# Projection first on SyncE's queue, warming operand set by VectorE, orders made anew

## The chip, the cores and the metric

The kernel runs on one core of one Trainium2 chip. The metric is device time in microseconds, the median of three executions. The core has five instruction streams that run in parallel and meet by semaphores: TensorE (PE: products; PEld: its weight loads), VectorE (DVE), ScalarE (ACT), GpSimd (POOL) and SyncE (SP), which here only issues transfers.

## What is computed

Attention in which a query sees only the keys of its own hash bucket, followed by a feed-forward layer with a squared ReLU:

```python
q_bits = (np.einsum('bhsd,dk->bhsk', q, proj) > 0).astype(np.int64)
k_bits = (np.einsum('bhsd,dk->bhsk', k, proj) > 0).astype(np.int64)
...
mask = q_bucket[:, :, :, None] == k_bucket[:, :, None, :]
scores = scale * np.matmul(q, k.transpose(0, 1, 3, 2))
scores = np.where(mask, scores, -1000000000.0)
...
attn = attn / (np.sum(attn, axis=-1, keepdims=True) + 1e-09)
return np.matmul(attn, v).astype(np.float32)
...
h = np.maximum(x @ w_in, 0.0)
return (h * h @ w_out).astype(np.float32)
```

Batch 4, 8 heads, 768 tokens, head size 64, 6 hash bits (`proj` is 64 x 6); 3072 tokens through 512 x 2048 x 512. All in float32.

## The kernel before

**Work.** A visit is one batch, one pair of heads and 384 queries; there are 32 visits of 6 units. A unit is 128 queries of one head against all 768 keys: TensorE makes the scores `pS`, in which the hash codes are extra rows of the product (tiles `A`, `L` against `Q`, `M`, or `arena` for batch 0); VectorE takes the maximum (`e<-pS`), ScalarE the exponential (`e<-e,maxes`) with its row sum in `sums`; the sum is inverted (`rv`). For the first five visits (`PLAIN_AV`, line 54) GpSimd multiplies by `rv` (`e<-e,rv`), TensorE transposes in six pieces of which three at a time lie in a bank (`bank<-unit_f,e`, `pT<-unit_f,e`), and ScalarE copies them out (`aT<-bank`, `aT<-pT`). For the others ScalarE and VectorE split the scaled row into two float16 parts (`hl`), and a transposing transfer brings it to `aT`. After six units TensorE multiplies with the values (`pA<-aT`), and the tile is copied out (`xx<-pA`). When the four pairs of heads of 384 tokens are there, `moe` (from line 1171) multiplies by the first weights (`bank<-xx,win`), squares (`g`), and multiplies by the second (`po<-wo,g`). The last batch goes through `strassen`, with fewer products.

**Setting up a pair of heads.** `prep` makes the hash codes `bits` (a product with the projection `pj`, compared with a threshold), scales `R` into `A`, makes `L`, copies a scaled half of `A` over its other half (`A<-A`, or `arena<-arena`, 64 x 768: the half copy; engines in `HALF_BY`, line 75), and puts the codes, 12 rows by 384, into `L` and `M` (`code`; engines in `CODE_BY`, line 75). The weights come in pieces of 512 columns: a transfer, then `top` on ScalarE, the bit merge `f` on VectorE, the high part `win<-f` or `wo<-f` and the low part `win<-f,win`.

**The start.** The first visit has a path of its own: keys `K` and queries `G` are loaded in halves (`T` and `U`), the projection `pj0` goes into `pj` and `wide_pj` on VectorE, and TensorE multiplies K and G by `wide_pj` (`pd<-K,wide_pj`, `pd<-G,wide_pj`). `GS` is G scaled by ScalarE; `pS<-K,GS` are the first scores. The transfers of this path stand in a list (lines 636 to 643) whose entries follow each other on each queue. Before them `emit` puts warming products `bank<-ones`, whose operand `ones` is filled by a memset, and more of them wherever the planned order leaves TensorE without work for long before the first feed-forward product (`fill`, from line 518).

**The order.** No order is written by hand: every operation is recorded by `Program.add`, and `Program.order` plays a list schedule with durations of its own (`cost`, `LAGS`, `PRICE`), taking ready operations by rank; where an operation may run on several engines, the one that would be done first takes it. `MOVES` is a table of 150 entries that shift ranks of stretches of the list. So a changed parameter or table changes the order on every engine. Lines 532, 536 and 539 are where `emit` issues warming products, grouped products and everything else, which is why almost every row of the profile has line 539.

Of the kernel before, what the change touches and what calls it, by code (L numbers as in the profile page):

```python
# [12 lines left out]
BF16 = mybir.dt.bfloat16  # L13
# [10 lines left out]
P = 128  # L24
B, H, S, D = 4, 8, 768, 64
NB = 6
# [15 lines left out]
PRICE = dict(pe=1, dve=4.53, act=0.28, pool=2.55, sp=6.14)  # L42
AHEAD, DELAY, LAG = 101, 21166, 1.0
# [4 lines left out]
PREP, STACKS, VALUES = -3, 2, 1  # L48
WIN_RANK, WOUT_RANK = (12, 3.1999999999999997), (27, 1.6)
# [11 lines left out]
EARLY_SUMS, SUMS_RANK, SUMS_AT = 24, 160, (68, 42)  # L61
VERIFY = (3, 7)

PT_TAGS = ('pm', 'po2')

WIN_AT, WOUT_AT = (0, 1), 0
FIRST = len(WIN_AT)

PACE = ((16, 0), (64, 141), (96, 277), (125, 480), (157, 537), (188, 622))

TOP_BY, LOW_BY = ('act',), ('dve',)
RUN = 18
MERGED, TOGETHER, PAIRED = 0, 1, 0
LANES = 8
CODE_BY, HALF_BY, WIDE, KM = (('dve', 'gp'), ('sp',)), ('dve',), 1, 76
# [7 lines left out]
IDLE_FROM, IDLE_FIRST, IDLE_SHARE, IDLE_UNTIL = 1000, 36, 0.6, 18000  # L83
# [477 lines left out]
def run(ctx: ExitStack, tc, kq, v, proj2, w_in, w_out, consts, out, flag):  # L561
    fast = flag is not None
# [5 lines left out]
    pr = Program(tc)  # L568
# [50 lines left out]
    cst = sb([P, 4], F32, "cst")  # L619
    if not fast:  # L620
        sp.dma_start(cst, consts[:, 0:4])
    pj = sb([P, 32], F32, "pj")
    dve.memset(pj, 0.0)
    ones = sb([P, P], BF16, "ones")
    (pool if fast else dve).memset(ones, 1.0)
# [60 lines left out]
    for x in tops:  # L686
        dve.memset(x.bitcast(F32), 0.0)
# [728 lines left out]
```

## Time and profile before

| | |
|---|---|
| three executions | 790.21, 790.21, 790.88 us, median 790.21 |
| the profiled execution | 792.51 us, its span 790.4 us |
| granted TensorE clock | 0.999 of full |
| TensorE (PE) busy | 773.9 us, 98% |
| VectorE (DVE) busy | 644.8 us, 82% |
| ScalarE (ACT) busy | 621.3 us, 79% |
| GpSimd (POOL) busy | 273.0 us, 35% |

The span goes from the first to the last instruction of the profiled execution; 2.11 us of its time lie outside. Busy times are of one engine; in a row with a time in brackets the engine stood idle before that instruction, and what ended the wait stands behind the arrow. Instructions of one engine overlap slightly, so that the distance of two starts is shorter than the length shown.

### The profile page before, as it was taken

The numbers are of one execution on the slowest core, as the hardware profiler recorded it, in microseconds if no ns is written. First come the engines' busy times: TensorE is split into PE (matmuls) and PEld (weight loads), VectorE is DVE, ScalarE is ACT, GpSimd is POOL, SyncE is SP. The second block draws the span as 40 slices with busy tenths as digits, with TensorE's granted clock in tenths as the row PEclk, the third lists the DMA queues.
The fourth block names the chain that finished last, engine by engine and source line by source line (L and its number), as shares of the span: only waits on it lengthen the run. The fifth ranks groups of instructions, "written<-read, shape, count | busy, mean of one in ns | idle before, by whom it ended". The sixth has DMA issues, their size and how long they took to land.

```text
span 790.4 us, 14405 instructions
## 1 busy us (share of the span) xinstructions
PE 773.9 (98%) x4893; PEld 421.9 (53%) x4893; DVE 644.8 (82%) x1265; ACT 621.3 (79%) x1164; POOL 273.0 (35%) x357
## 2 busy tenths in 40 slices
PE   8999999999999999999999999999999999999996
PEld 5555645555555555555555555545555555545553
DVE  6999999989999889888888888888988546967462
ACT  6999999999889889989888897979867779432211
POOL 3766422433414242441415243233582011320000
PEclk9999999999999999999999999999999999999999
DMA  7876699999999999999999989988626698830002
GB/s 227 255 222 194 195 239 191 224 200 191 184 190 184 190 182 193 203 192 185 191 191 196 179 176 207 183 164 167 114 41 141 174 291 256 258 101 0 1 1 84
DMA packets 286273, 137.41 MB, mean 174 GB/s; under 512 B 258912, under 2 KB 266352, under 8 KB 286192
## 3 DMA queue, kind: packets, MB, share of 16 engines
q1 hardware_dynamic: 285856, 135.99, 76.9%
q8 instruction: 40, 0.66, 0.3%
q10 hardware_dynamic: 304, 0.43, 0.2%
q14 instruction: 41, 0.34, 0.1%
q0 software_dynamic: 32, 0.01, 0.0%
HBM read 56.36 MB, written 6.29 MB: 79 GB/s over the span
## 4 chain that ended last, share of the span: by engine, by line
PE 87%; DVE 5%; ACT 4%; issue 2%; DMA 2%; POOL 0%; DVEq 0%; ACTq 0%; POOLq 0%
PE po L539 26%; PE bank L539 26%; PE pS L539 16%; PE pA L536 11%; PE pn L539 3%; DVE e L539 2%; ACT e L539 1%; PE pA L539 1%; PE pd L536 1%; DMA aT<-hl 1%; DVE f L539 1%; ACT aT L539 1%; DVE hl L539 1%; ACT hl L539 1%; PE bank L532 1%
## 5 line engine op out<-in xcount | busy, mean ns | idle before, releaser
L539 PE MATMUL bank<-xx,win 128*128 128x384 f16 x1152 | 229.7, 326 | 0.6 <-ACT g L539 0.6
L539 PE MATMUL po<-wo,g 128*128 128x512 f16 x864 | 229.3, 379 | 0.0
L539 DVE TENSOR_SCALAR_CACHE_REDUCE e<-pS 128x768 f32<-128x768 f32 x192 | 182.7, 953 | 32.0 <-PE pS L539 27.4
L539 ACT ACTIVATE e<-e,maxes 128x768 f32<-128x768 f32 x192 | 178.7, 932 | 26.0 <-DVE e L539 23.7
L539 DVE SCALAR_TENSOR_TENSOR hl<-e,rv,hl 128x768 f16<-128x768 f32 x162 | 171.8, 1065 | 12.6 <-ACT hl L539 11.9
L539 PEld LDWEIGHTS <-win 128*128 128x128 f16 x1296 | 125.8, 97 | 100.6 <-issue 3.9
L539 ACT ACTIVATE hl<-e,rv 128x768 f16<-128x768 f32 x162 | 149.3, 924 | 7.2 <-DMA aT<-hl 5.1
L539 PEld LDWEIGHTS <-g 128*128 128x128 f16 x864 | 83.8, 97 | 81.6 <-issue 2.1
L539 POOL TENSOR_SCALAR rv<-sums 128x1 f32<-128x1 f32 x111 | 31.5, 284 | 234.3 <-ACT e L539 194.3
L539 ACT ACTIVATE g<-g 128x384 f32<-128x384 f32 (+1 forms) x179 | 91.9, 514 | 4.0 <-PE po L539 2.3
L536 PE MATMUL pA<-aT,VV 128*64 128x384 f16 x972 | 84.5, 327 | 0.6 <-DMA aT<-hl 0.6
L539 PE MATMUL pS<-A,Q 128*128 128x384 f16 x324 | 82.0, 327 | 2.4 <-DVE e L539 2.4
L539 POOL TENSOR_TENSOR g<-g,g 128x384 f16<-128x384 f32 x57 | 61.6, 1082 | 62.7 <-ACT g L539 39.1
L539 PE MATMUL pS<-L,M 76*128 76x384 f16 x324 | 82.1, 326 | 0.0
L539 ACT ACTIVATE g<-bank 128x384 f32<-128x384 f32 x96 | 46.3, 482 | 30.3 <-PE bank L539 27.8
L536 PEld LDWEIGHTS <-VV 128*64 128x64 f16 x972 | 53.3, 110 | 30.8 <-issue 9.6
L539 PEld LDWEIGHTS <-Q 128*128 128x128 f16 x324 | 29.8, 98 | 34.8 <-issue 12.8
L539 ACT ACTIVATE gq<-y 128x384 f16<-128x384 f32 x32 | 16.1, 520 | 39.5 <-DVE y L539 39.5
L539 PEld LDWEIGHTS <-gq 128*128 128x128 f16 x288 | 28.1, 98 | 30.8 <-issue 0.2
L539 PEld LDWEIGHTS <-M 76*128 76x128 f16 x324 | 31.7, 98 | 22.9 <-issue 1.2
L539 PE MATMUL po<-wo,gq 128*128 128x512 f16 x144 | 42.4, 379 | 0.0
L539 POOL COPY L<-bits 12x384 f16<-12x384 f16 x52 | 33.5, 645 | 17.5 <-DMA Q<-L 14.0
(132 smaller groups left out, 1021.5 us busy)
## 6 DMA issues: line engine op xcount, KB each, us to landing
R<-kq SPq DMA_DIRECT2D x32, 384.0 KB
X<-kq SPq DMA_DIRECT2D x32, 384.0 KB
wo<-w_in SPq DMA_DIRECT2D x16, 511.8 KB
V<-vp SPq DMA_DIRECT2D x19, 384.0 KB
X<-vp SPq DMA_DIRECT2D x16, 384.0 KB
wo<-w_out SPq DMA_DIRECT2D x12, 511.8 KB
out<-o SPq DMA_DIRECT2D x23, 256.0 KB
Q<-A SPq DMA_DIRECT2D x28, 96.0 KB
```

What stands on the lines that cost most here:

```text
L532: issue(q, q.engine.matmul(self.idle[0].real(), self.idle[1].real(), self.idle[1].real(), start=True, stop=True).ins)
L536: ins = q.engine.matmul(*map(real, args), **kw).ins
L539: ins = getattr(q.engine, o.name)(*map(real, o.args), **{k: real(x) for k, x in o.kw.items()}).ins
```

## The change

The list of the first transfers becomes a string for each queue: ScalarE's queue now issues only one half of the keys, SyncE's the projection (p), the other half of the keys (T), the unit matrix (i) and both halves of the queries (t, u). GpSimd issues none. The operand of the warming products is filled by VectorE, and the other memsets of VectorE come after it. The code copies into `L` go to ScalarE alone; the half copies may go to VectorE or GpSimd. The other parameters, and `MOVES` in all its lines, are new numbers.

```diff
-PRICE = dict(pe=1, dve=4.53, act=0.28, pool=2.55, sp=6.14)
-AHEAD, DELAY, LAG = 101, 21166, 1.0
+PRICE = dict(pe=1, dve=4.53, act=0.28, pool=2.55, sp=2.93)
+AHEAD, DELAY, LAG = 68, 21136, 1.0
-PREP, STACKS, VALUES = -3, 2, 1
-WIN_RANK, WOUT_RANK = (12, 3.1999999999999997), (27, 1.6)
+PREP, STACKS, VALUES = -3, 1, 5
+WIN_RANK, WOUT_RANK = (11, 3.7999999999999994), (27, 1.9)
-EARLY_SUMS, SUMS_RANK, SUMS_AT = 24, 160, (68, 42)
+EARLY_SUMS, SUMS_RANK, SUMS_AT = 26, 230, (68, 48)
-PT_TAGS = ('pm', 'po2')
-WIN_AT, WOUT_AT = (0, 1), 0
+PT_TAGS = ('po2', 'pm')
+WIN_AT, WOUT_AT = (1, 1), 1
-PACE = ((16, 0), (64, 141), (96, 277), (125, 480), (157, 537), (188, 622))
+PACE = ((15, 0), (64, 135), (103, 283), (125, 474), (153, 537), (188, 637))
+FIRST_LOADS = (('act', 'U'), ('sp', 'pTitu'))
-CODE_BY, HALF_BY, WIDE, KM = (('dve', 'gp'), ('sp',)), ('dve',), 1, 76
+CODE_BY, HALF_BY, WIDE, KM = (('act',), ('sp',)), ('dve', 'pool'), 1, 76
-IDLE_FROM, IDLE_FIRST, IDLE_SHARE, IDLE_UNTIL = 1000, 36, 0.6, 18000
+IDLE_FROM, IDLE_FIRST, IDLE_SHARE, IDLE_UNTIL = 1000, 34, 0.6, 18000
 MOVES = (
-    (120397674, 0, -721062, -717689, 8884), (747214626, 1, -342155, -336385, 6372), (0, 2, 1388, 1388, 1156),
+    (366631055, 0, -697903, -686703, 1673), (364062845, 0, -456146, -452977, 2935), (297115142, 0, -455454, -453992, 7434),
...
     pj = sb([P, 32], F32, "pj")
+    ones = sb([P, P], BF16, "ones")
+    dve.memset(ones, 1.0)
     dve.memset(pj, 0.0)
-    ones = sb([P, P], BF16, "ones")
-    (pool if fast else dve).memset(ones, 1.0)
...
-        for q, to, src in (
-            (pool, pj0[:, 0 : 3 * NB], proj2[:, NB : 4 * NB]),
-            (sp, K0[T], kq[b0, 2 * hp0, T, 0:S]),
-            (act, K0[U], kq[b0, 2 * hp0 + 1, T, 0:S]),
-            (sp, unit_f, consts[:, 4 + 2 * P :]),
-            (act, G0[U], kq[b0, 2 * hp0 + 1, U, 0:n0]),
-            (sp, G0[T], kq[b0, 2 * hp0, U, 0:n0]),
-        ):
+        operands = {
+            "p": (pj0[:, 0 : 3 * NB], proj2[:, NB : 4 * NB]),
+            "T": (K0[T], kq[b0, 2 * hp0, T, 0:S]),
+            "U": (K0[U], kq[b0, 2 * hp0 + 1, T, 0:S]),
+            "t": (G0[T], kq[b0, 2 * hp0, U, 0:n0]),
+            "u": (G0[U], kq[b0, 2 * hp0 + 1, U, 0:n0]),
+            "i": (unit_f, consts[:, 4 + 2 * P :]),
+        }
+        for q, (to, src) in [(getattr(pr, k), operands[x]) for k, line in FIRST_LOADS for x in line]:
...
+    if fast:
+        for o in pr.ops[1:]:
+            if o.ways[0][0] is dve and o.ways[0][1] == "memset":
+                o.after.add(0)
```

What this makes of the order, at three places. SyncE's queue at the start, before (`K` and `G` keys and queries, `unit_f` the unit matrix, `R` the next heads, `wo<-w_in` weights in passing):

```order
L539 DMA K<-kq 64x768
L539 DMA unit_f<-consts 128x128
L539 DMA G<-kq 64x384
L539 DMA R<-kq 128x768 x2
L539 DMA wo<-w_in 128x2047 x3
L539 DMA Q<-A 64x768
L539 DMA Q<-L 64x768
```

SyncE's queue at the start, in the changed kernel:

```order
L540 DMA pj_71<-proj 128x18
L540 DMA K<-kq 64x768
L540 DMA unit_f<-consts 128x128
L540 DMA G<-kq 64x384 x2
L540 DMA R<-kq 128x768
L540 DMA wo<-w_in 128x2047
L540 DMA R<-kq 128x768
L540 DMA wo<-w_in 128x2047 x2
```

The projection stands first; the keys' half is second, and both halves of the queries are fourth and fifth, where one was third. One load of `R` has gone behind a load of weights.

VectorE's first instructions before:

```order
L539 MEMSET marks 64x1
L539 MEMSET wide_pj 128x128
L539 MEMSET pj 128x32
L539 MEMSET marks 64x1 x3
L539 MEMSET top_83 128x512
L539 MEMSET top_89 128x512
L539 TENSOR_SCALAR pj<-pj_71 128x2x6
L539 TENSOR_SCALAR pj<-pj_71 128x12
L539 TENSOR_SCALAR wide_pj<-pj 128x12 x2
```

VectorE's first instructions in the changed kernel:

```order
L540 MEMSET ones 128x128
L540 MEMSET pj 128x32
L540 MEMSET wide_pj 128x128
L540 MEMSET marks 64x1 x3
L540 MEMSET top_81 128x512
L540 MEMSET marks 64x1
L540 MEMSET top_85 128x512
L540 TENSOR_SCALAR pj<-pj_71 128x2x6
L540 TENSOR_SCALAR pj<-pj_71 128x12
```

A memset of `ones` stands at the head; the copies that wait for the projection follow the same memsets as before.

ScalarE from the first weight conversion, before (`aT` transposed copies, `arena` and `A` scaled heads, `top` a step of the weights):

```order
L539 ACTIVATE win<-f 128x512
L539 ACTIVATE top_83<-wo 128x512
L539 ACTIVATE aT<-bank 128x3x128
L539 ACTIVATE aT<-pT 128x3x128
L539 ACTIVATE e,sums<-e,maxes 128x768 x2
L539 ACTIVATE aT<-bank 128x3x128
L539 ACTIVATE aT<-pT 128x3x128
L539 ACTIVATE arena<-R,marks 128x768
L539 ACTIVATE win<-f 128x512
L539 ACTIVATE arena<-R,marks 128x768
```

ScalarE from the first weight conversion, in the changed kernel:

```order
L540 ACTIVATE win<-f 128x512
L540 ACTIVATE top_81<-wo 128x512
L540 ACTIVATE L<-bits 12x384 x2
L540 ACTIVATE aT<-pT 128x3x128
L540 ACTIVATE aT<-bank 128x3x128
L540 ACTIVATE e,sums<-e,maxes 128x768 x2
L540 ACTIVATE aT<-bank 128x3x128
L540 ACTIVATE L<-bits 12x384
L540 ACTIVATE arena<-R,marks 128x768 x2
L540 ACTIVATE L<-bits 12x384
```

Four code copies `L<-bits` stand between the same kinds of instructions, one of the transposed copies is missing (VectorE makes it), and two scalings into the arena follow each other. Over the whole order ScalarE gets 64 code copies (GpSimd had 60, VectorE 4), GpSimd gets 16 of the 32 half copies that were all VectorE's, and five transposed copies go from ScalarE to VectorE. TensorE has 88 warming products, in pieces of 34, 9, 12, 3, 17 and 13, in place of 62 in pieces of 36, 14 and 12; its other products are the same in number.

## Rows read from the trace of the kernel before

**Rows 1.** The page, busy time of each engine over the span.
```profile
PE 773.9 (98%) x4893; PEld 421.9 (53%) x4893; DVE 644.8 (82%) x1265; ACT 621.3 (79%) x1164; POOL 273.0 (35%) x357
```

**Rows 2.** Busy time by stretch, all engines: stretch, length, then busy time and count each.
```profile
10.00:20.00 10.00, 9.64 (x78) 5.53 (x76) 9.40 (x22) 8.01 (x17) 5.19 (x8) 1.00 0.72 201
20.00:80.00 60.00, 54.35 (x362) 32.38 (x359) 55.12 (x122) 59.35 (x127) 40.41 (x54) 1.00 0.75 226
...
130.00:500.00 370.00, 369.99 (x2464) 200.08 (x2462) 325.17 (x653) 331.26 (x597) 131.57 (x181) 1.00 0.96 192
```

**Rows 3.** The start in order of time, all engines: start, length, instruction, idle time before it.
```profile
0.75 0.60 SPq L539 DMA_DIRECT2D K<-kq  x1
...
2.25 0.48 SPq L539 DMA_DIRECT2D G<-kq  x1
...
2.28 4.02 PE L532 MATMUL bank<-ones 128*128 128x128 bf16 x36 [2.28 <-POOL ones L539]
...
5.33 0.25 DVE L539 TENSOR_SCALAR pj<-pj 128x12 f32<-128x12 f32 x2 [2.92 <-DMA pj<-proj]
...
6.09 2.33 PE L539 MATMUL pd<-K,wide_pj 128*128 128x384 f32 x4
...
6.49 0.52 ACT L539 ACTIVATE GS<-G 128x384 f32<-128x384 f32 x1 [3.01 <-DMA G<-kq]
...
8.26 0.81 PE L539 MATMUL pd<-G,wide_pj 128*128 128x384 f32 x2
...
9.00 1.57 PE L536 MATMUL pS<-K,GS 64*128 64x384 f32 x6
```

**Rows 4.** DMA issues: queue, count, size, microseconds from issue to landing.
```profile
pj<-proj POOLq DMA_DIRECT2D x1, 9.0 KB, 4.0
```

**Rows 5.** Groups by form on GpSimd, VectorE, TensorE: count, busy us, mean ns, idle before.
```profile
L539 POOL COPY L<-bits 12x384 f16<-12x384 f16 x52 | 33.5, 645 | 17.5 <-DMA Q<-L 14.0 <-POOL rv L539 0.8
...
L539 DVE SCALAR_TENSOR_TENSOR f<-wo,top 128x512 uint32<-128x512 uint32 x28 | 20.8, 747 | 0.3
...
L539 DVE TENSOR_SCALAR A<-A 64x768 f16<-64x768 f16 x28 | 13.4, 477 | 0.8
L539 DVE SCALAR_TENSOR_TENSOR xx<-pA,xx 128x384 f16<-128x384 f32 x24 | 13.1, 546 | 2.4 <-ACT xx L539 2.3
...
L539 DVE TENSOR_SCALAR rv<-sums 128x1 f32<-128x1 f32 x81 | 12.1, 149 | 11.7 <-ACT e L539 10.5
...
L539 DVE COPY L<-bits 12x384 f16<-12x384 f16 x4 | 1.0, 253 | 0.1
...
L539 PE MATMUL bank<-xx,win 128*128 128x384 f16 x1152 | 229.7, 326 | 0.6 <-ACT g L539 0.6
```

**Rows 6.** The half copy on VectorE: shortest, median and longest ns, first and last start.
```profile
L539 DVE TENSOR_SCALAR A<-A x28: 350/354/1199, 18.1 to 533.2; 64x768 f16<-64x768 f16 x28
```

**Rows 7.** ScalarE in order of time, at three places between 33 and 86 us.
```profile
33.56 0.96 ACT L539 ACTIVATE arena<-R,marks 128x768 f16<-128x768 f32 x1
...
78.34 0.54 ACT L539 ACTIVATE xx<-pA 128x384 f16<-128x384 f32 x1
...
83.63 0.63 ACT L539 ACTIVATE win<-f 128x512 f16<-128x512 f32 x1
84.15 0.53 ACT L539 ACTIVATE g<-g 128x384 f32<-128x384 f32 x1
84.56 0.49 ACT L539 ACTIVATE aT<-pT 128x384 f32<-128x384 f32 x1
84.93 0.79 ACT L539 ACTIVATE top<-wo 128x512 f16<-128x512 bf16 x1
85.57 0.52 ACT L539 ACTIVATE g<-g 128x384 f16<-128x384 f32 x1
```

**Rows 8.** TensorE in order of time, two products after a wait.
```profile
123.31 2.95 PE L536 MATMUL pA<-aT,VV 128*64 128x384 f16 x34 [0.57 <-DMA aT<-hl]
...
517.62 0.48 PE L539 MATMUL pS<-A,Q 128*128 128x384 f16 x2 [0.68 <-DVE e L539]
```

98 rows, old and new, of the table MOVES are left out of this document.

## The prediction

> **What bounds the kernel now.** I read the page first, then the busy time by stretch, then the first microseconds in order of time, then the rows before the few waits of TensorE. On the page the reader is to see that TensorE is busy 773.9 of 790.4 us [rows 1]: all that the change can win lies in the 16.5 us without a product and in products that do no work. The stretches and the start say where those are [rows 2, 3]: 2.28 us before the first product, 0.36 in the second ten microseconds, 5.65 between 20 and 80 us, 0.01 from 130 to 500. Single waits of 0.57 and 0.68 stand out later [rows 8]; most of the rest follows the last product, in the way out that the change does not touch. The first 36 products warm the engine and do no work, so the first useful product, the projection of the keys, starts at 6.09 us and the first scores at 9.00 [rows 3].
>
> So two things set the end: when the start chain lets the first scores begin, and how fast ScalarE and VectorE bring batch 0 to its first feed-forward product. Between 20 and 80 us ScalarE is busy 59.35 of 60 and VectorE 55.12 [rows 2]; the fourth attention tile leaves PSUM at 78.34 [rows 7], and the feed-forward products that then fill TensorE follow within a microsecond. From there TensorE is full.
>
> **The start.** Before, the projection comes by GpSimd's queue, 4.0 us from issue to landing [rows 4], and VectorE waits for it, 2.92 us, until 5.33 [rows 3]. Afterwards SyncE issues it at 0.75, where it issued half of the keys. With the same 4.0 it lands at 4.75. VectorE's four small copies and the step to TensorE, from 5.33 to 6.09 here, put the key product at 5.5. That would be 0.6 earlier, if the keys are there. Their SyncE half now starts one issue later: 0.60 by the row of its own issue [rows 3], so about 1.4. No row shows when keys land before; the bounds are 1.4 + 3.5, half a microsecond under the 4.0, and 1.4 + 5.3, since they were used at 6.09 after an issue at 0.75. So the product starts between 4.9 and 6.7, against 6.09. I take 5.5, near the 4.0 of the one measured landing.
>
> The second half of the queries, now SyncE's fifth transfer, decides next. ScalarE waited for the queries until 6.49, with the last of them issued at 2.25 [rows 3], 4.2 us. Two issues took 1.5 there (0.75 to 2.25), so with two more of 0.5 to 0.6 the fifth starts near 3.4 and lands near 7.6. Then the query product (0.81 us) ends at 8.4 and the scores begin there instead of at 9.00. **Term: -0.6 us**, between +0.5 and -1.3.
>
> The memset moves from GpSimd, for which the warming products waited until 2.28 [rows 3], to VectorE's first instruction, so they begin near 1.05, after one short instruction; 34 at 0.112 each (4.02 for 36 [rows 3]) end before 5. That by itself is worth nothing: the engine waits for keys then. Between the real products the order now has 54 warming products in place of 26. They stand where the new order expects gaps, and TensorE has 5.65 us of gaps between 20 and 80 [rows 2]. Cost nothing; without that cover 28 x 0.112 = 3.1 us at most.
>
> **A rule against the first part.** The row shows 4.0 us for 9 KB through GpSimd's queue [rows 4], and nothing of how the same 72-byte rows behave on SyncE's. The Trainium skill, page "DMA: Bandwidth & Descriptors", section Specifications, gives 512 B as the least transfer for line rate. By it the 128 short rows, now ahead of the keys in the same queue, could hold them up by more than one issue, and the term would be nearer to its slow end; no run here shows it.
>
> **Code copies onto ScalarE.** 64 copies of 12 x 384, of which GpSimd did 60, at 645 ns for the commoner form, and VectorE 4 at 253 [rows 5], all go to ScalarE. No row shows them there, so those two bound one. ScalarE's nearest row, the same 384 columns on all partitions, takes 0.41 from start to start (84.15 to 84.56 [rows 7]); I take that. I count both orders up to the fourth tile's copy. More: 16 code copies (6.6) and 2 tops at 0.64 (1.3). Less: 2 scalings into the arena at 0.96 (1.9), 5 transposed copies at 0.37 (1.9) and 6 weight conversions at 0.52 (3.1) [rows 7], where only the 0.96 is a length and the others are start to start. Sum +1.0; at 0.253 or 0.645 for a code copy, -1.6 or +4.7. It need not lie on the path: ScalarE had 1.99 us idle in the second ten microseconds [rows 2], and beyond the first attention tile both orders give it the same sum within 0.3. Term 0, between -1.6 and +4.7 less those 2.0, so +2.7.
>
> **VectorE.** To the same tile it gets 5 of the transposed copies (0.546 each by its own PSUM row), 3 more bit merges (0.747), 8 more adds of a row sum (0.149), and loses 3 half copies (0.477) [rows 5]: 2.7 + 2.2 + 1.2 - 1.4 = +4.7. It has 4.9 us idle in 20 to 80 [rows 2], so it fits, but barely. To the last split before the first transposed attention products (those that waited until 123.31 [rows 8]) it is +8.0 in the same way, mostly weight work done earlier: 10 row-sum adds, 4 bit merges, 5 transposed copies and 5 more of about half a microsecond, less 4 half copies. Ahead of them now stand 15 more products, at 0.199 (229.7 us over 1152 [rows 5]) 3.0 us. So 5.0 us must come out of VectorE's idle time. Term 0, between -0.6, a fifth of 28 x (0.477 - 0.354) [rows 5, 6], and +5.0.
>
> **Later.** TensorE's waits of 0.57 and 0.68 us [rows 8] were made by this order and go with it; others may come. ScalarE has some 39 us idle between 130 and 500 [rows 2], so the other 48 code copies (20 us) have cover; without it they would cost what lies behind one copy, 0.4 each. GpSimd loses some 60 x 0.645 = 39 us and takes 16 half copies. Term -0.3, between -1.25 and +0.7 (one wait of that size more).
>
> **Sum.** -0.6 + 0 + 0 - 0.3 = -0.9 us. The profiled execution took 792.51, 2.11 over its span, and stands 2.3 above the median of 790.21; against the span it is 789.5, against the median **789.3 us**.
>
> **Rivals.** *VectorE becomes the bound (slower).* The 5.0 us before the first transposed products do not find their idle time, because VectorE's gaps lie in places that wait for TensorE or ScalarE, and the first feed-forward stage starves. It decides when VectorE can use less than half of its 4.9 us. With 40% used, 5.0 - 1.9 - 0.6 = +2.5: 792.7 us. For it: 55.12 of 60 busy, the wait at 123.31. Against: the weight work comes earlier, so later stages owe less. Chance 0.16.
>
> *The early stage tightens (faster).* The start reaches its good end (-1.3), both waits go (-1.25): 787.7 us. The rows bear it in that VectorE's half copy, 354 ns in the middle of its rows and 1199 at worst, averages 477 [rows 5, 6], so something holds it up; half of these copies leave VectorE and 60 small copies leave GpSimd. The Trainium skill, page "SBUF — State Buffer", section Who interferes with whom, says that VectorE in its two-port modes, or with two inputs in SBUF, and GpSimd lock each other out of a shared pair of ports for a whole instruction. By that rule less GpSimd work shortens VectorE's rows, here by those 0.6 us in the early stage. The 477 against 354 agrees with it, and no row here isolates it. Chance 0.36. Against it: TensorE can't do more than the scores and attention products that exist before 78 us.
>
> *The start does not move.* The keys arrive at 6.1 or later, because the small transfer is ahead of them; the gain is zero to +0.5 and the time, with the -0.3, 789.9 to 790.4. Chance 0.10.
>
> **How the numbers follow.** What a measurement can tell from no change here is about 0.2%, 1.6 us: 788.6 to 791.8. The forecast has 0.38; with the start that does not move, also inside, that makes 0.48; faster 0.36; slower 0.16. The range reaches from 787.0, a little past the faster rival, to 792.4, most of the way to the slower one. What is left out is some 0.08 below and 0.10 above.
>
> **What would show it.** Right: warming products from about 1.1 us; VectorE's wait for the projection ends near 4.8; first scores at 8.4; ScalarE's code copies near 0.4 us; the first feed-forward product within a microsecond of 78.5; TensorE without gaps from 130 to 500. The start is wrong if the key product waits past 6.0, the cover of VectorE is wrong if it is idle less than 2 us in 20 to 80 and TensorE more than 6.5. The whole is wrong if gaps over a microsecond appear after 130 us, or if the last copies of the output, untouched here, move.

## The result: 798.09 us against 790.88

The changed kernel takes 798.09 us in the median of six executions (797.02 to 800.93), the kernel before 790.88 beside it: a ratio of 1.0096, 95% interval 1.0077 to 1.0116. It is slower by some 7 us, where 789.3 was forecast. Its profiled execution took 797.02 with a span of 795.1; before, 792.51 and 790.4. So the profile of the change shows the shortest of its six executions, and that of the kernel before one longer than any of the six beside it (790.21 to 792.31): the two profiles hold only 4.5 of the 7.2 us between the medians.

The page first, the same row as [rows 1]:

```profile
PE 775.3 (98%) x4919; PEld 420.5 (53%) x4919; DVE 647.1 (81%) x1286; ACT 643.5 (81%) x1208; POOL 236.4 (30%) x291
```

GpSimd has 36.6 us less and ScalarE 22.2 more. TensorE's busy time grew by 1.4 us, the span by 4.7. The busy time by stretch, as [rows 2]:

```profile
10.00:20.00 10.00, 8.63 (x72) 4.74 (x72) 8.93 (x23) 9.86 (x19) 4.34 (x5) 1.00 0.95 298
20.00:80.00 60.00, 53.14 (x373) 31.17 (x373) 51.33 (x127) 58.95 (x124) 37.68 (x45) 1.00 0.66 205
130.00:500.00 370.00, 368.19 (x2446) 198.66 (x2442) 327.81 (x664) 344.74 (x626) 91.34 (x130) 1.00 0.97 188
```

Columns are length, then TensorE, its loads, VectorE, ScalarE and GpSimd, granted clock, DMA share and GB/s. TensorE's gap in 20 to 80 us is 6.86 us instead of 5.65, and between 130 and 500 there now is 1.81 where there was 0.01. VectorE is emptier than before (8.67 us idle in 20 to 80), so it did not become the bound. ScalarE lost the room that it had in the second ten microseconds: 9.86 busy instead of 8.01.

The start, in order of time, answers to [rows 3]:

```profile
0.74 0.40 SPq L540 DMA_DIRECT2D pj<-proj  x1
...
1.06 3.81 PE L533 MATMUL bank<-ones 128*128 128x128 bf16 x34 [1.06 <-DVE pj L540]
...
3.00 0.25 DVE L540 TENSOR_SCALAR pj<-pj 128x12 f32<-128x12 f32 x2 [0.47 <-DMA pj<-proj]
...
5.11 1.53 PE L540 MATMUL pd<-K,wide_pj 128*128 128x384 f32 x4 [0.24 <-DMA K<-kq]
...
7.21 1.57 PE L537 MATMUL pS<-K,GS 64*128 64x384 f32 x6
```

The start went better than forecast. The projection is used 2.3 us after its issue, and the first scores begin at 7.21 instead of 9.00. Part of it is TensorE's clock: its first record of 1.00 in the trace is at 4.9 us, before the change at 7.7, and the key products take 1.53 us instead of 2.33. How much of the 1.8 us is the clock's, other profiles show (in the part on why the prediction was wrong).

So 1.8 us were won by 7 us, and yet the first feed-forward product comes 2.3 us late, at 81.45 instead of 79.14, first before and then after the change:

```profile
79.14 0.33 PE L539 MATMUL bank<-xx,win 128*128 128x384 f16 x1
```

```profile
81.45 0.32 PE L540 MATMUL bank<-xx,win 128*128 128x384 f16 x1
```

The last product ends at 787.47 instead of 784.13, and the way out after it takes 7.63 us instead of 6.26. Of the 4.7 us between the two profiled spans 3.3 lie ahead of the last product and 1.4 behind it. What TensorE waits for, over the whole span (us in total, times, longest), lines from before and then the longest of the changed kernel:

```profile
PE bank L539 <- ACT aT L539: 1.7, 3, 0.8
...
PE bank L539 <- ACT g L539: 0.6, 2, 0.4
...
PE pT L539 <- ACT aT L539: 0.5, 1, 0.5
PE bank L532 <- ACT aT L539: 0.3, 1, 0.3
```

```profile
PE pT L540 <- ACT aT L540: 3.7, 6, 1.0
PE bank L533 <- ACT aT L540: 3.3, 3, 1.1
PE pS L540 <- DVE e L540: 1.5, 4, 0.5
...
PE po L540 <- DVE rv L540: 0.9, 1, 0.9
```

For `aT` TensorE waited 2.5 us in all before, and now 7.0 in the first two lines. `aT` is ScalarE's copy of a group of transposed probabilities out of PSUM: the next transposes wait for it, and so do warming products that write the same PSUM bank. Here is ScalarE's timeline at one place of that stage, with two of the code copies that the change put there, and then their group by form (count, busy us, mean ns, idle before):

```profile
18.42 0.47 ACT L540 ACTIVATE aT<-bank 128x384 f32<-128x384 f32 x1
18.91 0.52 ACT L540 ACTIVATE L<-bits 12x384 f16<-12x384 f16 x1
19.45 1.76 ACT L540 ACTIVATE arena<-R,marks 128x768 f16<-128x768 f32 x2
21.24 0.52 ACT L540 ACTIVATE L<-bits 12x384 f16<-12x384 f16 x1
21.79 0.78 ACT L540 ACTIVATE top<-wo 128x512 f16<-128x512 bf16 x1
...
23.34 0.47 ACT L540 ACTIVATE aT<-pT 128x384 f32<-128x384 f32 x1
23.71 0.93 ACT L540 ACTIVATE e<-e,maxes 128x768 f32<-128x768 f32 x1
```

```profile
L540 ACT ACTIVATE L<-bits 12x384 f16<-12x384 f16 x56 | 29.1, 520 | 1.3
```

A code copy of 12 rows takes 0.54 us from start to start (18.91 to 19.45, 21.24 to 21.79; the median of all 56 is 0.544), a transposed copy of 128 rows 0.37 (23.34 to 23.71). The forecast had taken 0.41.

### The profile page after: what moved, and what is told of

It reads as the page before. It is cut to its first block, busy times and chain, and to the rows that moved or that the text cites. A ratio compares the mean times of both kernels' runs of the same rounds, so it can differ in the third digit from the quotient of the medians.

```text
span 795.1 us, 14437 instructions
## 1 busy us (share of the span) xinstructions
PE 775.3 (98%) x4919; PEld 420.5 (53%) x4919; DVE 647.1 (81%) x1286; ACT 643.5 (81%) x1208; POOL 236.4 (30%) x291
## 4 chain that ended last, share of the span: by engine, by line
PE 80%; DVE 4%; ACT 3%; DMA 1%; issue 1%; DVEq 0%; ACTq 0%; SPq 0%
PE po L540 25%; PE bank L540 25%; PE pS L540 15%; PE pA L537 10%; PE pn L540 3%; PE pA L540 1%; PE pd L537 1%; DVE hl L540 1%; ACT e L540 1%; DVE e L540 1%; DMA aT<-hl 1%; ACT g L540 1%; DVE VV L540 1%; ACT hl L540 1%; DMA wo<-w_out 0%
## 5 line engine op out<-in xcount | busy, mean ns | idle before, releaser
L540 DVE TENSOR_SCALAR_CACHE_REDUCE e<-pS 128x768 f32<-128x768 f32 x192 | 182.7, 952 | 24.2 <-PE pS L540 18.7
L540 ACT ACTIVATE hl<-e,rv 128x768 f16<-128x768 f32 x160 | 147.5, 923 | 2.8 <-DVE rv L540 1.8
L540 POOL TENSOR_SCALAR rv<-sums 128x1 f32<-128x1 f32 x90 | 27.8, 308 | 243.9 <-ACT e L540 218.7
L540 ACT ACTIVATE g<-g 128x384 f32<-128x384 f32 (+1 forms) x175 | 90.1, 516 | 4.1 <-PE po L540 2.3
L540 POOL TENSOR_TENSOR g<-g,g 128x384 f16<-128x384 f32 x45 | 43.1, 957 | 68.2 <-ACT g L540 47.6
L540 DVE SCALAR_TENSOR_TENSOR g<-g,g 128x384 f16<-128x384 f32 x51 | 31.1, 610 | 22.8 <-ACT g L540 22.0
```

What stands on the lines that cost most here:

```text
L540: ins = getattr(q.engine, o.name)(*map(real, o.args), **{k: real(x) for k, x in o.kw.items()}).ins
```

## Experiments

Three theories were set against one another. COPIES: ScalarE is full before the first feed-forward product, so the code copies push back what TensorE waits for. BLOCKS: late warming products stand behind transposes, wait for ScalarE's copy of them and hold up all that is behind. ORDER: the order made anew is slower in itself. A fourth came up at the way out: CODE PLACE.

A planner makes the order anew from any change of the source. To take out one part alone, each kernel below replays an order: the place and the engine of every operation are written down from the kernel before or from the changed one and not planned again, and only what the diff shows differs. `WAY` is the engine of an operation, `FILL` says how many warming products stand ahead of which matrix operation.

| run | median us (range) | ratio to before (95%) | first feed-forward product | last product ends | way out |
|---|---|---|---|---|---|
| before | 790.88 to 791.56 in five batches | 1 | 79.14 | 784.13 | 6.26 |
| the change | 798.09 (797.02 to 800.93) | 1.0096 (1.0077 to 1.0116) | 81.45 | 787.47 | 7.63 |
| head_alone | 791.94 (789.75 to 793.27) | 1.0004 (0.9994 to 1.0015) | 78.67 | 783.87 | 6.26 |
| before_few | 791.34 (790.10 to 792.23) | 0.9996 (0.9987 to 1.0006) | 78.74 | 783.37 | 6.51 |
| copies_added | 814.01 (812.80 to 816.31) | 1.0288 (1.0271 to 1.0304) | 90.98 | 806.25 | 6.15 |
| relief | 790.91 (790.28 to 792.49) | 0.9997 (0.9988 to 1.0006) | 78.34 | 782.17 | 6.30 |
| relief_head | 791.56 (791.00 to 792.96) | 1.0006 (0.9997 to 1.0015) | 79.23 | 783.39 | 5.99 |
| few_warm | 798.49 (797.64 to 800.04) | 1.0089 (1.0074 to 1.0104) | 82.81 | 789.79 | 7.63 |
| codes_back | 795.18 (794.39 to 795.66) | 1.0044 (1.0030 to 1.0057) | 80.93 | 785.32 | 7.72 |
| both_back | 796.79 (796.30 to 797.93) | 1.0073 (1.0059 to 1.0086) | 81.47 | 787.16 | 7.63 |
| tail_shift | 796.74 (795.20 to 797.94) | 1.0066 (1.0052 to 1.0080) | 82.04 | 787.91 | 6.13 |
| blocks_ahead | 797.40 (796.37 to 798.91) | 1.0073 (1.0060 to 1.0087) | 83.18 | 789.45 | 7.54 |
| head_undone | 798.94 (796.66 to 799.05) | 1.0094 (1.0079 to 1.0110) | 81.32 | 787.28 | 7.60 |
| codes_back_tail | 794.17 (791.91 to 794.49) | 1.0032 (1.0020 to 1.0044) | 79.48 | 783.88 | 6.04 |
| repaired_again | 793.50 (792.45 to 794.80) | 1.0027 (1.0018 to 1.0036) | 79.61 | 784.32 | 6.21 |
| repaired_few | 795.34 (794.80 to 795.51) | 1.0045 (1.0032 to 1.0058) | 79.79 | 787.18 | 6.28 |
| repaired_old_head | 794.72 (793.06 to 795.02) | 1.0033 (1.0021 to 1.0045) | 82.18 | 786.47 | 6.84 |

The three columns on the right are of the one profiled execution of each, and single executions of one kernel differ by up to 4 us; a difference under 1 us there is not read, and one of 1 to 3 us between two profiles is a hint and no measure. The batches ran on different chips, each with the kernel before beside it. Against the median of that, the change is 7.2 us slower, codes_back 4.0, tail_shift 5.4, codes_back_tail 2.7 and repaired_again 1.9.

### The head alone

```diff
-FILL = [(21, 36), (54, 12), (62, 14)]
+FILL = [(21, 34), (54, 12), (62, 14)]
+FIRST_LOADS = (('act', 'U'), ('sp', 'pTitu'))
...
-    dve.memset(pj, 0.0)
...
-    (pool if fast else dve).memset(ones, 1.0)
+    dve.memset(ones, 1.0)
+    dve.memset(pj, 0.0)
```

> The kernel before, with its order of instructions on every engine held fixed, and only the new head: the new first transfers, the ones set by VectorE's first memset, 34 first warming products. Three theories stand. BLOCKS: the time went because late warming products stand behind transposes and wait, with everything behind them, until ScalarE has emptied the bank that they share. COPIES: ScalarE has too much to do before the first feed-forward product, with 16 of the 12-row copies at 0.52 us there. ORDER: the rest of the new order is slower whatever the head. By BLOCKS, COPIES and ORDER alike the head is good: first scores at 7.2 us instead of 9.0, last product some 1 to 1.8 us earlier than 784.13, time 789.0 to 790.0. If the head itself cost the time (its transfers push the weights back), it would be 793 or more.

No difference can be told: 1.0004, although the first scores begin at 7.11. ScalarE's timeline, first before and then here, shows where the gain goes:

```profile
9.55 0.78 ACT L539 ACTIVATE top<-wo 128x512 f16<-128x512 bf16 x1 [0.41 <-DMA wo<-w_in]
11.97 0.94 ACT L539 ACTIVATE e<-e,maxes 128x768 f32<-128x768 f32 x1 [1.64 <-DVE e L539]
```

```profile
10.91 0.78 ACT L554 ACTIVATE top<-wo 128x512 f16<-128x512 bf16 x1 [1.59 <-DMA wo<-w_in]
11.56 0.91 ACT L554 ACTIVATE e<-e,maxes 128x768 f32<-128x768 f32 x1
```

Before, the first weights came at 9.55 and were prepared while ScalarE waited for scores. Now the scores come 1.9 us earlier, but the weights, behind two more transfers of SyncE's queue, 1.4 later, and the first exponential starts only 0.41 earlier. From there on ScalarE is full: by 34 us it is 0.38 ahead, at the first feed-forward product 0.47, less than is read here. The expectation of 1 to 1.8 us was wrong.

### Late warming products left out, of the changed kernel and of the old one

```diff
-FILL = [(21, 34), (41, 12), (62, 9), (92, 3), (105, 17), (349, 13)]
+FILL = [(21, 34)]
```

> The changed kernel with the same order, but of the warming products only the first 34; the 54 between real products are left out (they compute nothing that is used). BLOCKS: the waits of 1.13, 1.12 and 1.05 us before such blocks and the 2.0 us that the three blocks run are gone; at least half of it reaches the end: last product at 783 to 785.5 instead of 787.5, first feed-forward product at 79.0 to 80.0 instead of 81.45, time 792 to 795. COPIES: the next real product waits for the same copies of ScalarE, so no more than 1 us: last product after 786.5, time 796.5 to 798. ORDER: as COPIES, 0 to 1 us. A cost of leaving them out would show as a granted clock below 1.00 before 80 us.

No gain, so BLOCKS falls as it was put. The warming products' waits are gone, but TensorE's waits for the copies on `pT` rose from 3.7 to 4.8 us, and the granted clock was 0.50, that is 1.2 of 2.4 GHz, for 6.8 us (the column ahead of the last two):

```profile
22.00:24.00 2.00, 1.01 (x7) 0.39 (x4) 1.85 (x3) 1.98 (x5) 0.00 (x0) 1.00 0.28 70
24.00:26.00 2.00, 1.59 (x10) 0.98 (x10) 1.71 (x3) 2.00 (x5) 0.89 (x2) 1.00 0.77 232
26.00:28.00 2.00, 0.78 (x5) 0.69 (x4) 1.63 (x5) 2.00 (x6) 1.72 (x3) 0.52 0.96 322
28.00:30.00 2.00, 2.00 (x9) 1.19 (x8) 1.02 (x3) 1.85 (x5) 1.17 (x2) 0.50 0.70 219
30.00:32.00 2.00, 2.00 (x10) 1.67 (x9) 0.85 (x4) 1.16 (x3) 1.60 (x2) 0.50 0.16 35
32.00:34.00 2.00, 2.00 (x13) 1.37 (x13) 2.00 (x4) 1.54 (x4) 1.07 (x2) 0.77 0.26 64
```

TensorE had been busy 2.60 of the 4 us before; the changed kernel with its warming products kept 1.00 through this stretch in its profiled execution. Nor does the clock alone hide a gain: the two executions without them whose mean clock was 0.998 took 797.64 and 798.09, the three of the change at 0.998 took 797.24 to 798.40. So what the waits of the warming products had cost, the next transposes took, and in three of five executions (mean clock 0.993 and 0.994) the clock fell besides.

The same for the kernel before, `FILL` to `[(21, 36)]`:

> The kernel before with its order held fixed, without its 26 later warming products, a control for the run above. BLOCKS: there one of the two blocks waited 0.25 us for a copy of ScalarE and the blocks ran 0.85 and 0.89 us, so up to 1 us less: 789.5 to 790.9, last product 783.2 to 784.1. COPIES and ORDER: no change, 790.2 to 791. A loss above 1 us, or a granted clock below 1.00 in the first 80 us, would show that the later warming products earn their time.

No difference (0.9996), and the clock stayed at 1.00. There the 26 products neither cost nor earn anything.

### The code copies, back on GpSimd and then added alone

In the changed kernel, with `WAY` of the 64 copies set to GpSimd, and then the reverse in the kernel before, with `WAY` set to ScalarE:

```diff
-CODE_BY = (('act',), ('sp',))
+CODE_BY = (('dve', 'gp'), ('sp',))
```

> The changed kernel with the same order, but the 64 copies of 12 rows from ScalarE back on GpSimd, each at its place in the order. COPIES: ScalarE gets back 16 x 0.52 = 8.3 us before the first feed-forward product; its copies of the transposed probabilities come earlier, the waits of TensorE for them (3.7 us on pT, 3.3 on warming products) shrink by half or more: first feed-forward product before 80.0, time 793 to 795.5. BLOCKS: the waits shrink by what stands directly ahead of the three copies only, the blocks themselves stay: 796 to 798. ORDER: no more than 1 us, 796.5 to 798.5; or slower, where the copies are late on GpSimd.

```diff
-CODE_BY = (('dve', 'gp'), ('sp',))
+CODE_BY = (('act',), ('sp',))
```

> The kernel before, its order held fixed, with one part of the change alone: the 64 copies of 12 rows go from GpSimd (60) and VectorE (4) to ScalarE, each at its place in the order. COPIES (ScalarE is full before the first feed-forward product, so each copy there pushes what stands behind it): some 16 x 0.52 us more work for ScalarE before that product against 2.0 us of idle time, so the first feed-forward product at 81 to 85 instead of 79.14 and the time 793 to 797. ORDER (the copies only hurt where the new order puts them, the old one has room): 790 to 791.5, first feed-forward product before 79.8.

COPIES holds; ORDER had left the copies at most 1 us. Without the copies on ScalarE the change costs 0.44% instead of 0.96%: 2.9 us less between the medians, 3.2 against the kernel before beside each. TensorE's waits for the copies on `pT` fell from 3.7 to 1.3 us; those of the warming products hardly did (3.3 to 3.1), and the first feed-forward product came at 80.93, not before 80.0 as COPIES had it:

```profile
PE bank L547 <- ACT aT L554: 3.1, 3, 1.3
...
PE pT L554 <- ACT aT L554: 1.3, 2, 0.8
```

Added alone to the old order the copies cost 22.6 us, far more than the 2 to 6 of the expectation. The first feed-forward product then starts 11.8 us late,

```profile
90.98 0.33 PE L553 MATMUL bank<-xx,win 128*128 128x384 f16 x1
```

though 16 x 0.54 = 8.7 us is all that the copies ahead of it last (a part is the clock's, at 0.50 for 6.8 us from 26.0 and 3.4 from 70.4), and another 10 us are lost later, where ScalarE had been idle a tenth of the time. TensorE's waits for ScalarE rose from 1.7 to 7.4 us for `aT` and from 0.6 to 4.5 for `g`:

```profile
PE bank L553 <- ACT aT L553: 7.4, 10, 1.6
PE bank L553 <- ACT g L553: 4.5, 5, 1.3
```

So the copies stand ahead of what TensorE waits for, and ScalarE's idle time lies elsewhere. The new order loses 3 us to the copies and not 23; that it places most of them better is the likely reason, which no run isolates.

### The half copies back as well

```diff
-CODE_BY, HALF_BY = (('act',), ('sp',)), ('dve', 'pool')
+CODE_BY, HALF_BY = (('dve', 'gp'), ('sp',)), ('dve',)
```

> The changed kernel with its order, the 64 copies on GpSimd again as in the run before, and also the 16 half copies from GpSimd back on VectorE: what is left of the change is the head, the parameters, the order and the warming products. HALVES (a half copy takes GpSimd 0.94 us against 0.40 on VectorE and the query transfer behind it waits): 792 to 794, below the 795.2 of the run that moved only the 12-row copies. ORDER (the rest of the loss lies in the order and in the way out): 794.5 to 796.5.

Slower by 1.6 us than with the code copies alone, and 0.3 over the range of ORDER. So HALVES falls: in this order the sixteen half copies are better on GpSimd.

### SyncE's last instructions

```diff
     if not fast:
-        sp.dma_start(cst, consts[:, 0:4])
+        for _ in range(24):
+            sp.dma_start(cst, consts[:, 0:4])
```

> The changed kernel, its order held fixed, with 24 small transfers more in the program for unusual inputs that stands behind the fast one and is branched over: nothing more is executed, but SyncE's last instructions lie elsewhere in its code. The way out took 7.63 us after the last product instead of 6.26, of which 1.60 is one gap between two of SyncE's last waits that began right where a load of instructions began. CODE PLACE: that gap is gone or falls ahead of the branch; the way out is 6.0 to 6.5 us, the time 796.0 to 797.2 against 798.1. If the gap is a wait for the outputs' transfers it stays: way out 7.4 to 7.8, time 797.5 to 798.7. Last product at 787 to 788 by both.

CODE PLACE holds. The way out took 6.13 us and the median fell to 796.74 (5.4 us over the kernel before beside it, where the change is 7.2 over), with nothing else executed. The view of the instructions at the program's end shows the gap in the changed kernel, in two neighbouring windows, 791 to 793.8 and 793.8 to 794.3 us: SyncE's waits on semaphores, first and last start.

```profile
L1418 SPq EVENT_SEMAPHORE  x2: 28/28/28, 792.2 to 792.3; - x2
...
L1418 SPq EVENT_SEMAPHORE  x6: 27/28/28, 793.9 to 794.2; - x6
```

Two of 28 ns, then 1.60 us of nothing, then six more in 0.3 us. No transfer of outputs lands then; the trace has packets of the instruction queue from 792.4 on. The kernel before has no such gap. All six profiles of the new order without the extra code have one at this place, of 1.34 to 1.60 us, and none of the five with it does. The Trainium skill, page "Runtime: NRT & Kernel Launch", section Instruction fetch mechanics, says that a taken branch out of the loaded pages stalls until its target is fetched, and that crossing a block is mostly hidden. The trace agrees on the branch (2.9 and 3.1 us of nothing follow it on SyncE, after the change and before) and shows one more stop ten waits behind it, of 1.60 us, that is not hidden; that a block is crossed there is likely by the packets, and not shown.

### The blocks ahead of the transposes

```diff
-FILL = [(21, 34), (41, 12), (62, 9), (92, 3), (105, 17), (349, 13)]
+FILL = [(21, 34), (41, 12), (45, 3), (62, 9), (88, 17), (248, 13)]
```

> The changed kernel with its order and all its 88 warming products, but the three blocks of 3, 17 and 13 stand ahead of the group of three transposes that they stood behind, so that they no longer wait for ScalarE's copy of that group. Without the blocks the granted clock was 0.50 from 26.1 to 32.9 us and nothing was gained. BLOCKS with the clock as their benefit: clock 1.00 throughout, no wait of a warming product over 0.6 us, the first feed-forward product at 80.0 to 81.0 and the time 795.5 to 797.5. COPIES alone: the transposes behind wait for the same copies, first feed-forward product at 81.2 to 81.7, time 797.5 to 798.7.

797.40 lies where the two ranges meet and the first feed-forward product (83.18) outside both, with the granted clock at 0.50 from 24.2 to 27.6 us in the profiled execution, so not 1.00 throughout. TensorE's waits for the copies on `pT` rose to 5.5 us. With the copies on ScalarE, where the blocks stand, and whether, is worth a microsecond at most.

### Both repairs, and the old head in the new order

`CODE_BY` back and the 24 transfers, together:

> The changed kernel, its order held fixed, with the two repairs that each gained alone: the 64 copies of 12 rows on GpSimd again (795.2 instead of 798.1) and the 24 transfers in the program that is branched over (796.7, way out 6.13 instead of 7.63). COPIES and CODE PLACE as separate causes: the gains add up, 793.4 to 794.2, way out 6.0 to 6.5, last product at 785 to 786; what is left to 791.2, some 2.6 us, is then of the order. If the two are one and the same cause: 794.8 to 796.

The medians add up within the expectation (794.17). The profiled execution is the shortest of the six, 791.91, and its last product ends at 783.88, ahead of the 785 to 786 expected. Its first feed-forward product starts at 79.48, against 82.04 with the way out repaired alone; the other such pair, codes_back and the change, has 80.93 and 81.45, so that single profiles do not say what the copies cost by then.

```diff
-FIRST_LOADS = (('act', 'U'), ('sp', 'pTitu'))
+FIRST_LOADS = (('pool', 'p'), ('sp', 'Tit'), ('act', 'Uu'))
...
-    dve.memset(ones, 1.0)
+    (pool if fast else dve).memset(ones, 1.0)
```

> The changed kernel, its order held fixed, with the old head: the projection by GpSimd's queue, half of the queries by ScalarE's, the ones set by GpSimd; 34 first warming products. STAGE FULL (ScalarE and VectorE are full until 80 us, so that what the start gains is used up by 30 us whatever the order, as in the run of the head alone: 1.9 us at the first scores, 0.47 at the first feed-forward product, nothing in the median): first scores at 8.7 to 9.0, first feed-forward product at 81.4 to 82.0, time 797.8 to 798.8. If the new order was made for the early start and needs it: first feed-forward product at 82.5 to 83.5 and the time 799 to 800.5.

798.94 and 81.32: no difference that can be told, as STAGE FULL had it. The first scores came at 7.60, not at 8.7 or later. GpSimd here sets the ones ahead of its transfer and so at 0.75, which is not the old head in all respects; but the same edit in repaired_old_head below gave first scores at 9.82. The first record of full clock stands at 4.15 us in the one profile and at 9.68 in the other.

### Room on ScalarE in the kernel before

`WAY` of four weight conversions from ScalarE to GpSimd, `win<-f` at 20 and 35 us and `wo<-f` at 43 and 50, alone and with the head:

```diff
-WAY[158], WAY[168], WAY[173], WAY[178] = act, act, act, act
+WAY[158], WAY[168], WAY[173], WAY[178] = pool, pool, pool, pool
```

> The kernel before, its order held fixed, with four weight conversions of ScalarE (three for the second half of the first 40 us and one at 50 us; 0.52 us of its time each) done by GpSimd at the same places. STAGE FULL with ScalarE as the bound: ScalarE gets back 2.1 us before the first feed-forward product, which starts at 77.0 to 78.5 instead of 78.7 to 79.1; time 788.8 to 790.5. If VectorE, or GpSimd by its scaled probabilities that now come later, is the bound: no change or up to 1 us slower, 790.8 to 792.4.

> The relief of the run above and the new head together, on the order of the kernel before. STAGE FULL with ScalarE as the bound: with room on ScalarE the early start is worth more than the 0.47 us that it was worth alone; first feed-forward product at 76.0 to 77.8, time 787.8 to 789.6, the fastest of all. If another engine is the bound: as the head alone, 78.4 to 78.9 and 790.8 to 792.2.

Neither gains: 0.9997 alone and 1.0006 with the head. ScalarE was 1.2 to 1.9 us less busy between 20 and 80 us (58.10 and 57.45), the first feed-forward product came within 0.8 us of before, and the time is the same. So more work on ScalarE costs time, but less of it gains none, and room there does not turn the early start into time. Which engine binds then was not isolated. No version here beats the kernel before.

### What is left

With both repairs the ratio is still 1.003. Three runs asked for its cause.

> The changed kernel with both repairs (the 64 copies on GpSimd, 24 transfers more in the program that is branched over), a second time, for its spread: it took 794.2 us in the median and 791.9 in the profiled execution, whose last product ended at 783.9, as before the change. ORDER (the remaining 2.5 us lie in the same places of the order in each execution): median 793.4 to 794.6, last product at 785 to 786.5. FIRST LOADS (they depend on when the first keys and weights land): again a spread of over 2 us, with places before 30 us where executions differ by 1 us.

> Both repairs, and of the warming products only the first 34. LATE WARMING PRODUCTS as what is left: with the copies off ScalarE their waits (0.63, 0.73 and 1.05 us, and 2 us of running) are no longer covered by other waits of ScalarE's copies; 791.5 to 793, provided that the granted clock stays at 1.00 through 24 to 33 us. If it falls there as in the run without them before: 793.8 to 795. ORDER or FIRST LOADS: 793.4 to 794.6.

> Both repairs, and the old first transfers: the projection by GpSimd's queue, half of the queries by ScalarE's, with the ones set by GpSimd ahead of its transfer. FIRST LOADS as what is left (SyncE's queue now issues two transfers more ahead of the first keys of the next pair and the first weights, for which ScalarE waits): 791.6 to 793. ORDER: 793.4 to 794.8, as the head made no difference to the whole change (798.9 with the old head).

A second time it took 793.50 (792.45 to 794.80). Its profiled execution (792.61) again ends its last product (784.32) where the profiled one of the kernel before did (784.13), ahead of the range of ORDER; but that one took 792.51, more than the median of its kernel, so that these two profiles do not hold what the medians differ by. The spread of 2.35 us is as FIRST LOADS had it; yet with the old first transfers the kernel is no faster (794.72), which is in the range of ORDER. Without the late warming products it is slower than all three had it (795.34), in the profile at a granted clock of 1.00.

A part of the rest goes with the clock. Of the 18 executions of this kernel, four had a mean granted clock of 0.995 and took 794.23 to 794.80; eight had 0.999 and took 791.91 to 793.95. A mean of 0.995 is some 7 us or more at 0.50, longer than the whole way out, where the clock falls in every profile; none of 69 executions of the kernel before had a mean under 0.997. The eight have a median of 792.9, against 791.2 of the kernel before at 0.999 and over: some 1.7 us stay in the order without it. Where they lie is open.

## Why the prediction was wrong

**The step that failed is the code copies: "Term 0, between -1.6 and +4.7 less those 2.0, so +2.7".** The mechanism was there, its size was set to nothing. The price was 0.41, measured 0.54: for 16 copies 2.1 us more, which makes the sum of that step +3.1 instead of +1.0. The cover of 2.0 us in the second ten microseconds was taken as free for any instruction; it was used up there (ScalarE busy 9.86 of 10), and what was left over lay on the path, as taking the copies off shows. Undone alone, they give back 2.9 us of the median (3.2 against the kernel before beside each), a little above the upper bound of that term. The rival that was thought the slow one, VectorE, did not come: it fitted its work and idled 8.67 us.

**The start.** -0.6 was forecast at the first scores and -1.8 measured between the two profiles. The projection was used 2.3 us after its issue and not 4.0. But the 9.00 of the kernel before is a late one: with the same transfers the profiles of before_few, relief and copies_added have 8.64, 8.48 and 7.90, and the four follow the first record of full clock (7.75, 7.02, 6.70 and 5.51 us). With the new transfers the first scores begin at 6.98 to 7.42 in all eleven profiles, with that record at 3.7 to 5.7. So 0.5 to 0.9 us remain against the earliest of the old ones, about the size forecast, and the rest goes with the clock. The prediction counted the earlier warming (1.06 instead of 2.28) as worth nothing. By the rule of the Trainium skill, page "DMA: Bandwidth & Descriptors", section Specifications, the keys behind 72-byte rows could have been held up; the trace shows no loss by it, they were used at 5.11 instead of 6.09. But the term was carried to the end undiminished, and that was wrong: alone it was worth 0.47 us at the first feed-forward product and nothing in the median. There the weights land 1.4 us later and ScalarE is busy 58.95 of 60 us, as the prediction's own row (59.35 of 60) let expect. That ScalarE is what uses the gain up is not shown: room on it did not release the gain (relief_head).

**Warming products** cost nothing, as forecast, though not for the reason given: they waited 3.3 us in their bank, and without them the next transposes waited for the same copies.

**Later.** The two old waits are gone and others came, the largest of 0.95 us at 308 in the second layer's products: 1.8 us of gaps between 130 and 500, where -0.3 was forecast for all that is later. That the 48 later copies "have cover" is refuted for the old order by the run that added them alone.

**The way out** was not in the sum, since the change does not touch it; it costs 1.4 us in the profiles by where the code lies. The prediction named moved output copies as a sign that it would be wrong as a whole.

**VectorE's rows** did get shorter, as the faster rival said: the half copy averages 399 ns instead of 477 and the bit merge 691 instead of 747 [rows 5], and 428 and 742 with the copies back on GpSimd. That agrees with the shared ports in the Trainium skill, page "SBUF — State Buffer", section Who interferes with whom. The run that only took the copies off GpSimd agrees for the half copy (390 ns) and not for the bit merge (763), so that the cause is not shown for both. No run isolates what the shorter rows were worth. (A fifth of 28 x 0.123 is 0.7 and not 0.6; nothing hangs on it.)

In sum, of the 7.2 us between the medians the runs give 3.2 to the code copies and 1.8 to the way out, undone one by one, and 4.5 to 5.3 to both together. The other 2 to 3 us are of the order, where the prediction allowed for 0.7 of new waits; where they lie, and which of the new parameters made them, is open. The distance of 8.8 us from the forecast has besides the 0.9 that were forecast as gains and did not come, and the 0.7 by which the kernel before itself stood higher beside the change (790.88 and not 790.21).

## What to carry to other kernels

Price a small instruction on an engine by a row of that very kind on that engine; where none exists, run the sum at the dear end of the bound when the engine is full. An idle share is no cover for work in a fixed order: ask which waited-for instruction stands behind each added one. A gain at the start counts only as far as the next engine without room; look there before carrying it into the sum, and compare the way out as well, since code that only moves can cost as much as an edit.

## What the hardware showed that was not expected

- A copy of 12 rows of 384 16-bit values on ScalarE takes 0.544 us from start to start, more than its copies of 128 rows of 384 32-bit values, 0.37 out of PSUM (`aT`) and 0.41 within SBUF (`g` in [rows 7]). Which of the differences does it was not tried.
- Late warming products hold TensorE's clock only sometimes: without them it was 0.50 for 6.8 us in one profile and 1.00 in the two others; placed elsewhere 0.50 for 3.4 us. The two longest executions of the change (799.85 and 800.93) had a mean clock of 0.993, the other four 0.997 or 0.998.
- SyncE's place in its code is worth some 1.4 us at the end: the six profiles of the new order without the extra code took 7.54 to 7.72 us to leave, the five with it 6.04 to 6.84.
